# Weight sums of batch 1 on VectorE inside its own first layer, and the rest of a first layer begun one gap earlier

## The chip, the cores and the metric

One core of one Trainium2 chip. The metric is the device time of one execution in microseconds (us). The engines are TensorE (PE; PEld is its weight load), VectorE (DVE), ScalarE (ACT), GpSimd (POOL) and SyncE (SP), which issues most DMAs. Each engine works through its own instructions in the order of the program and waits on semaphores for the others.

## What is computed

```
mask   = q_assign[:, :, :, None] == k_assign[:, :, None, :]   # 16 clusters a head
scores = where(mask, q @ k.T / 8, -1e9);  attn = softmax(scores)
x = (attn @ v).transpose(0, 2, 1, 3).reshape(3072, 512)       # 4 batches of 768 rows
h = x @ w_in                                                  # 512 x 2048
g = h * (1.0 / (1.0 + exp(-1.702 * h)))
out = g @ w_out                                               # 2048 x 512
```

q, k and v are (4, 8, 768, 64). The first layer of the feed-forward part is `x @ w_in` with its gelu, the second is `g @ w_out`.

## The kernel before

The attention of all 16 pairs of heads comes first (to 339.85 us). Then the four batches follow one another, a first and a second layer each, and TensorE's order is this order. The kernel writes every engine's order by hand: instructions run on an engine in the order in which the Python code issues them, and small generators (`nxt`, `more`, `rest`, `pend`) are advanced at chosen places so that VectorE's work falls between TensorE's products.

Both layers use seven products of sums in place of eight blocks (Winograd's form of Strassen's method). A product needs sums of weight blocks and sums of the moving operand, made beforehand by VectorE or GpSimd, and its result is added to or copied from a PSUM bank by VectorE (`add`, L884) and ScalarE (copies, gelus).

- **First layer, batch 0** (`first7`, L893): seven products for each f of 8. `sums_w` makes the weight sums S1, S2, S4 of a later f on GpSimd.
- **First layer, batch 1** (`first7_psum`, L928): for each of 8 steps n, with f = `TURN[n]`, seven products accumulate in three banks x, z, v: A11 to x (copied to g1), A12 to z (added by VectorE to g1), S2 onto x (copied by ScalarE), S1 to v (copied by ScalarE), S3 onto x (added), S4 onto v (added), A22 onto x. ScalarE's order in a step is: copy x, copy x, gelu of the sum with z, copy v, two gelus, the last gelu. `sums_w1(n + 2)` (L977) issues the three sums S2, S1, S4 of step n + 2, all on GpSimd; for n = 0 and 1 they go to tiles W and are issued in batch 0's first layer, for n = 2 to 7 into parts of Z2, Z1 and Z2 again, tiles that hold weight sums of the second layer at other times. In steps n = 2, 4, 6 and after the last, `inner_w` (L994) makes sums of those sums on VectorE, eight instructions, and stores them and the sums of the two steps before to DRAM (`kept_i`, L1017, four DMAs issued by SP), where batches 2 and 3 get them.
- **First layer, batches 2 and 3** (`first49`, products L1083 and L1128): two levels, 49 products. It leaves a generator `rest`: the last additions (L884) and gelus (L1068), in two steps. The first is one addition of G, four of banks m to G, and two gelus.
- **Second layer, all batches** (`second49`, L1253): seven outer products k, in `ORDER`, each of seven inner ones: 1 to bank x, 2 to bank z, 6 onto x, 5 to v, 7 onto x, 3 onto v, 4 onto x. After the first, ScalarE copies x (L1263); after the second VectorE adds z, then `extra(0)` is called; after 6 ScalarE copies x again (L1269), so that 7 can be added; after 7 and 3 come `extra(1)` and `extra(2)`. `extra` advances `nxt` (the temporaries t2, t1, t4 of the next outer product, on VectorE), `more`, and in the first outer product `rest`, at 0 and at 1.

GpSimd's order behind batch 0's first layer is: four sums of Y (outputs, 128x768) in batch 0's second layer, then the 18 sums of `sums_w1` for n = 2 to 7, then batch 1's sums of Y. The sums for n = 6 write blocks of Z2 that `inner_w` of step 4 has just had stored to `kept_i`.

`sums` (L618) is the helper that records every such sum, so its line is that of many instructions; the tile names tell them apart.

Of the kernel before, what the change touches and what calls it, by code (L numbers as in the profile page):

```python
# [38 lines left out]
def fast(  # L39
# [26 lines left out]
    nc = tc.nc  # L66

    B, H, S, D = q.shape
# [547 lines left out]
    def sums(engine, todo):  # L616
        for o, a, op, b in todo:
            engine.tensor_tensor(out=o, in0=a, in1=b, op=(  # L618
                ALU.add if op == "+" else ALU.subtract))
# [3 lines left out]
    def A_in(row, col, f):  # L623

        at = (row * FB + f) * P
        return w_in[:, 2 * col:2 * col + 2, at:at + P]
# [182 lines left out]
    def turn_w(i):  # L809
        a = W_of(i)  # L810
        sums(nc.vector, ((a(0, 1), a(0, 0), "-", a(0, 1)),))
# [71 lines left out]
    def add(o, p, a):  # L883
        nc.vector.tensor_tensor(out=o, in0=p, in1=a, op=ALU.add)  # L884
# [92 lines left out]
    def sums_w1(n):  # L977

        if n >= FB:
            return  # L980
        f = TURN[n]
        if n < 2:
            S = wq.tile([P, 3, 2, P], FP32, name="W")
        else:
            S = Zb[1 + n // 2 % 2][:, n % 2 * 6:n % 2 * 6 + 6].rearrange(
                "p (i c) n -> p i c n", c=2)
        w_of[FB + f] = {1: S[:, 0], 2: S[:, 1], 3: A_in(1, 0, f), 4: S[:, 2],
                        0: S}
        S = w_of[FB + f]
        A11, A12, A22 = A_in(0, 0, f), A_in(0, 1, f), A_in(1, 1, f)  # L990
        sums(nc.gpsimd, ((S[2], A22, "-", S[3]), (S[1], S[2], "+", A11),
                         (S[4], A12, "-", S[2])))

    def inner_w(j, S):  # L994

# [243 lines left out]
    def second49(k, extra, last):  # L1239

        i = ORDER[k]
        a, g, t, w = W_of(i), G_of(i), temps(k), W.pop(k)
        A = {1: a(0, 0), 2: a(1, 0), 3: w[:, 2], 4: a(1, 1), 5: w[:, 1],
             6: w[:, 0], 7: a(0, 1)}
        M = {1: g(0, 0), 2: g(1, 0), 3: g(1, 1), 4: t[4], 5: t[1], 6: t[2],
             7: t[3]}

        def bank_b():
            return ps_b.tile([P, 512], FP32, name="b")[:, 0:QT]

        def product(ps, n, start):
            for f in range(FQ):
                nc.tensor.matmul(out=ps, lhsT=A[n][:, f], rhs=M[n][:, f],  # L1253
                                 start=start and f == 0,
                                 stop=(f == FQ - 1), skip_group_check=True)

        y = Y[22] if i == 1 else ep.tile([P, 2, HALF], FP32, name="y")
        y11, y12, y21, y22 = (y[:, m, q * QT:(q + 1) * QT]
                              for m in range(2) for q in range(2))
        p5 = ep.tile([P, QT], FP32, name="p5")  # L1260
        x = bank_b()
        product(x, 1, True)
        nc.scalar.copy(y11, x)  # L1263
        z = bank_b()
        product(z, 2, True)
        add(y11, z, y11)
        extra(0)
        product(x, 6, False)
        nc.scalar.copy(y12, x)  # L1269
        v = bank_b()  # L1270
        product(v, 5, True)
        nc.scalar.copy(p5, v)
        product(x, 7, False)
        nc.scalar.copy(y22, x)
        add(y22, y22, p5)
        extra(1)
        product(v, 3, False)
        add(y12, v, y12)
        if i == 4:
            c = Y[21]  # L1280
            add(c[:, 0], y[:, 0], c[:, 0])
            add(c[:, 1, QT:], y22, c[:, 1, QT:])
            extra(2)
        product(x, 4, False)
        if i == 4:
            add(c[:, 1, 0:QT], x, c[:, 1, 0:QT])
            return
        nc.scalar.copy(y21, x)
        extra(2)
        pool = nc.vector if last and i in (5, 7) else nc.gpsimd  # L1290
        sums(pool, {1: (),
                    2: ((Y[11], y, "+", Y[22]),),
                    3: ((Y[12], y, "+", Y[22]),),
                    6: ((Y[12], y, "+", Y[12]), (Y[21], y, "+", Y[22])),
                    5: ((Y[12], y, "+", Y[12]), (Y[22], y, "+", Y[21])),
                    7: ((Y[22], y, "+", Y[22]), (Y[21], y, "+", Y[21]))}[i])
# [74 lines left out]
    def do(steps, n):  # L1371
        for _ in range(n):
            next(steps, None)
# [3 lines left out]
    for b in range(B):  # L1377
        if b == 1:
            done = None
            for n, f in enumerate(TURN):  # L1380
                made_w = w_of[FB + f][0]
                first7_psum(b, f, *XT)
                if n % 2 == 0 and done:
                    inner_w(*done)
                sums_w1(n + 2)
                if n:
                    after7(TURN[n - 1])
                if n % 2 == 0:
                    one = made_w
                else:  # L1390
                    done = f - FQ, (one, made_w)
                do(pend, 2)
            after7(FB - 1)
            inner_w(*done)
        if b > 1:
            rest = first49(*XT)
        for f in range(FB if b == 0 else 0):
            first7(b, f, *XT)
            if f + 2 < FB:
                sums_w(f + 2)  # L1400
            else:
                sums_w1(f + 2 - FB)
            if f:
                after7(f - 1)
            if b == 0 and f < 3:
                for n in range(3 * f, min(3 * f + 3, FB)):
                    sums_z((nc.gpsimd, nc.vector, nc.vector)[n % 3], n)
            if b == 0 and f in (3, 4):
                for i in ORDER[0:4] if f == 3 else ORDER[4:]:
                    turn_w(i)  # L1410
            if b == 0 and f >= 3:
                for k in {3: (0,), 4: (1, 2), 5: (3,), 6: (4,), 7: ()}[f]:
                    keep_w(k, spare_y())
                if 5 <= f < 7:
                    load_sums(f - 5)
        if b == 0:
            after7(FB - 1)
        if b:
            move_z(b, 0)
        if b < B - 1:  # L1420
            for h in range(2):
                for hp in range(HP):
                    x = xT_of[b + 1, h, hp] = xp.tile([P, HALF], FP32,
                                                      name="x")
            made = sums_x(b + 1)
        else:
            made = iter(())

        def stores(b, *todo, **how):
            for n in todo:  # L1430
                store(b, n, **how)
                yield

        def tail():
            store(b, 22)
            yield

        def chain(*todo):
            for steps in todo:
                yield from steps  # L1440

        def sums_of_x():
            for XT[:] in made:
                yield

        x_steps = sums_of_x()
        final = b == B - 1
        if b < 2:
            rest = iter(())

        for k in range(7):
            nxt = sums_t(k + 1) if k < 6 else iter(())
            more = {1: sums_G(6), 2: sums_G(5), 3: sums_G(4),
                    4: stores(b, 11), 5: stores(b, 12) if final else x_steps,
                    6: tail() if final else x_steps}.get(k, iter(()))
            if b == B - 1 and k < 2:
                test(k)
            if (b, k) == (B - 1, 6):
                is_bad = nc.values_load(bad[0:1, 0:1], min_val=0, max_val=1)

            def extra(at):
                if k == 0 and at < 2:
                    do(rest, 1)
                do(nxt, (2, 1, 1)[at])
                do(more, ((1, 0, 1) if final else (0, 4, 4))[at] if k == 6
                   else (0, 0, 4)[at] if k == 2 else (0, 2, 2)[at])

            second49(k, extra, b in (0, B - 1))
            if k < 5:
                load_sums(k + 2, b == 0 and k > 2)  # L1470
            elif b < B - 1:
                load_sums(k - 5)
            if k < 3 and not (k == 2 and b):
                move_z(b, k + (b > 0))
            if k == 2 and b < B - 1:
                for h in range(2):
                    for hp in range(HP):
                        nc.sync.dma_start(out=xT_of[b + 1, h, hp],
                                          in_=kept[b, h, hp])
            if k in (4, 5) and 0 < b < B - 1:  # L1480
                load_inner(k - 4)
        pend = () if final else stores(b, 12, 22, 21)
        if final:
            store_last(b)
# [439 lines left out]
```

## Time and profile before

| | us |
|---|---|
| runs of the kernel | 894.80, 894.53, 893.81, 894.86; median 894.67 |
| the profiled execution, its own time | 893.86 |
| its span, first to last instruction | 892.1 |

Stages by TensorE's timeline, with the busy time of each engine in them:

| stage | from | to | length | PE | DVE | ACT | POOL |
|---|---|---|---|---|---|---|---|
| attention | 0 | 339.85 | 339.85 | 337.53 | 299.21 | 238.31 | 313.07 |
| batch 0, first layer | 339.85 | 412.13 | 72.28 | 72.28 | 65.45 | 21.16 | 58.23 |
| batch 0, second layer | 412.13 | 481.25 | 69.12 | 64.71 | 63.33 | 12.23 | 24.27 |
| batch 1, first layer | 481.25 | 553.50 | 72.25 | 72.25 | 35.29 | 26.67 | 4.55 |
| batch 1, second layer | 553.50 | 617.36 | 63.86 | 63.86 | 58.97 | 11.36 | 20.92 |
| batch 2, first layer | 617.36 | 684.82 | 67.46 | 67.46 | 41.82 | 28.87 | 0.00 |
| batch 2, second layer | 684.82 | 750.58 | 65.76 | 63.94 | 60.57 | 13.17 | 20.90 |
| batch 3, first layer | 750.58 | 818.21 | 67.63 | 67.63 | 41.99 | 28.86 | 0.00 |
| batch 3, second layer and end | 818.21 | 892.10 | 73.89 | 65.09 | 59.12 | 14.11 | 11.60 |

The granted clock of TensorE is 0.998 of full speed over the span. A line of a timeline reads: start and duration in us, engine, line of the program, operation, output<-inputs by the names of the program's tiles, shapes, number of instructions merged, and in brackets the idle time of the engine just before with what ended it. Durations overlap a little, since an instruction begins before its forerunner has left the engine; distances from start to start are the pace. An engine that is idle costs nothing unless TensorE comes to wait for it.

### The profile page before, as it was taken

The numbers are of one execution on the slowest core, as the hardware profiler recorded it, in microseconds if no ns is written. First come the engines' busy times: TensorE is split into PE (matmuls) and PEld (weight loads), VectorE is DVE, ScalarE is ACT, GpSimd is POOL, SyncE is SP. The second block draws the span as 40 slices with busy tenths as digits, with TensorE's granted clock in tenths as the row PEclk, the third lists the DMA queues.
The fourth block names the chain that finished last, engine by engine and source line by source line (L and its number), as shares of the span: only waits on it lengthen the run. The fifth ranks groups of instructions, "written<-read, shape, count | busy, mean of one in ns | idle before, by whom it ended". The sixth has DMA issues, their size and how long they took to land.

```text
span 892.1 us, 18225 instructions
## 1 busy us (share of the span) xinstructions
PE 874.7 (98%) x6910; PEld 605.1 (68%) x6910; DVE 725.8 (81%) x1223; ACT 394.7 (44%) x868; POOL 453.5 (51%) x411
## 2 busy tenths in 40 slices
PE   8999999999999999999989999999999999999996
PEld 3444444444444445557987556999887999887996
DVE  4899898999999996998898445799665899665895
ACT  3677777777677774322112333112434212444211
POOL 6899999999999997694270001144000143000140
PEclk9999999999999999999999999999999999999999
DMA  9655566656655320034633331747501547501424
GB/s 179 126 108 105 104 121 146 138 134 137 139 130 122 87 67 19 0 118 158 227 110 114 74 121 71 283 142 267 172 24 48 165 143 265 172 25 48 165 75 108
DMA packets 183186, 110.49 MB, mean 124 GB/s; under 512 B 153528, under 2 KB 161712, under 8 KB 180528
## 3 DMA queue, kind: packets, MB, share of 16 engines
q1 hardware_dynamic: 182832, 109.09, 45.0%
q8 instruction: 57, 0.93, 0.5%
q14 instruction: 41, 0.34, 0.1%
q10 hardware_dynamic: 256, 0.13, 0.1%
HBM read 83.05 MB, written 26.14 MB: 122 GB/s over the span
## 4 chain that ended last, share of the span: by engine, by line
PE 92%; DVE 6%; issue 1%; ACT 0%; POOL 0%; DVEq 0%; ACTq 0%; POOLq 0%
PE b L1253 23%; PE s L492 14%; PE o L557 14%; PE b L1128 8%; PE b L928 8%; PE b L893 8%; PE m L1083 7%; PE s L515 3%; PE m L574 3%; DVE G L618 2%; PE m L348 1%; DVE E L618 1%; DVE G L884 1%; PE o L296 1%; DVE Wz L618 0%
## 5 line engine op out<-in xcount | busy, mean ns | idle before, releaser
L541 POOL TENSOR_TENSOR sum<-sum,A 128x384 f32<-128x384 f32 x252 | 265.3, 1089 | 23.3 <-ACT A L523 21.7
L618 POOL TENSOR_TENSOR Y<-y,Y 128x768 f32<-128x768 f32 x24 | 63.3, 2651 | 307.5 <-DVE y L884 277.0
L523 ACT ACTIVATE A<-s 128x768 f32<-128x768 f32 x192 | 146.2, 807 | 85.8 <-PE s L515 66.4
L492 PE MATMUL s<-T,T 64*64 64x384 f32 x1536 | 143.1, 487 | 0.0
L557 PE MATMUL o<-A,inv 64*64 64x384 f32 x1536 | 141.2, 483 | 0.0
L884 DVE TENSOR_TENSOR G<-b,G 128x384 f32<-128x384 f32 x128 | 68.4, 554 | 57.9 <-PE b L928 36.2
L492 PEld LDWEIGHTS s<-T,T 64*64 64x64 f32 x1536 | 54.9, 132 | 69.1 <-ACT A L523 35.8
L618 DVE TENSOR_TENSOR G<-G 128x768 f32<-128x768 f32 (+1 forms) x84 | 96.3, 1173 | 0.2
L557 PEld LDWEIGHTS o<-A,inv 64*64 64x64 f32 x1536 | 58.3, 133 | 38.4 <-issue 33.3
L1253 PE MATMUL b<-G,w_out 128*128 128x192 f32 x320 | 55.9, 326 | 0.0
L1253 PEld LDWEIGHTS b<-G,w_out 128*128 128x128 f32 x320 | 52.7, 190 | 1.1
L1141 ACT COPY G<-b 128x384 f32<-128x384 f32 x64 | 30.4, 479 | 52.2 <-PE b L1128 52.2
L1253 PE MATMUL b<-E,Wz 128*128 128x192 f32 x288 | 50.5, 327 | 2.1 <-DVE E L618 2.1
L1253 PEld LDWEIGHTS b<-E,Wz 128*128 128x128 f32 x288 | 47.2, 190 | 3.0 <-issue 1.8
L515 PE MATMUL s<-rows,rows 64*64 64x384 bf16 x720 | 45.5, 322 | 0.0
L515 PEld LDWEIGHTS <-rows 64*64 64x64 bf16 x720 | 23.0, 107 | 32.7 <-issue 32.6
L1253 PE MATMUL b<-G,Wz 128*128 128x192 f32 x224 | 41.0, 326 | 0.0
L1253 PE MATMUL b<-G,Z 128*128 128x192 f32 x224 | 39.0, 326 | 0.0
L618 POOL TENSOR_TENSOR Z<-w_in 128x256 f32<-128x256 f32 x6 | 6.3, 1057 | 63.3 <-DVE G L884 63.3
L541 POOL TENSOR_TENSOR sum<-A 128x384 f32<-128x384 f32 x32 | 37.2, 1186 | 0.0
L1253 PEld LDWEIGHTS b<-G,Wz 128*128 128x128 f32 x224 | 37.2, 190 | 0.0
L1253 PEld LDWEIGHTS b<-G,Z 128*128 128x128 f32 x224 | 36.8, 190 | 0.0
(237 smaller groups left out, 1713.5 us busy)
## 6 DMA issues: line engine op xcount, KB each, us to landing
Wz<-kept_w SPq DMA_DIRECT2D x78, 256.0 KB
Z<-kept_z SPq DMA_DIRECT2D x9, 1024.0 KB
raw<-in_moe_w_in_dram SPq DMA_DIRECT2D x16, 512.0 KB
raw<-in_moe_w_out_dram SPq DMA_DIRECT2D x16, 512.0 KB
Z<-kept_i SPq DMA_DIRECT2D x8, 1024.0 KB
inv<-in_v_dram SPq DMA_DIRECT2D x16, 384.0 KB
in<-in_q_dram SPq DMA_DIRECT2D x60, 96.0 KB
in<-in_k_dram SPq DMA_DIRECT2D x60, 96.0 KB
```

The lines of the kernel that those rows point to most:

```text
L492: nc.tensor.matmul(out=ps[c:c + D, a, 0:HALF], lhsT=T[p, 1][rows, kt * P + c:kt * P + c + D], rhs=T[p, 0][rows, h * HALF:(h + 1) * HALF], ...
L515: nc.tensor.matmul(out=s_of[u][c:c + D, a, :], lhsT=rows_of[1, p % 2][rows, kt * P + c:kt * P + c + D], rhs=rows_of[0, p % 2][rows, h * HA ...
L523: nc.scalar.activation(out=A_of[u], in_=s_of.pop(u), func=AF.Exp, scale=SCALE)
L541: nc.gpsimd.tensor_tensor(out=sum_of[g][:, a], in0=(A_of[u - 1] if kt == 1 else sum_of[g])[:, a], in1=A_of[u][:, a], op=ALU.add)
L557: nc.tensor.matmul(out=o_of[g][a * D:(a + 1) * D, r, 0:HALF], lhsT=v_in[p][rows, a, kt, :], rhs=A[rows, a, :], start=(kt == 0), stop=(kt = ...
L618: engine.tensor_tensor(out=o, in0=a, in1=b, op=(ALU.add if op == "+" else ALU.subtract))
L884: nc.vector.tensor_tensor(out=o, in0=p, in1=a, op=ALU.add)
L893: nc.tensor.matmul(out=ps[:, 0:HALF], lhsT=a[:, c], rhs=x(c), start=(c == 0), stop=(c == 1))
L928: nc.tensor.matmul(out=ps, lhsT=a[:, c], rhs=x(c), start=start and c == 0, stop=(c == 1), skip_group_check=True)
L1083: nc.tensor.matmul(out=whole_of[j][m][:, 0:HALF], lhsT=a[:, c], rhs=x(c), start=n == 1 and c == 0, stop=c == 1, skip_group_check=True)
L1128: nc.tensor.matmul(out=ps[i][:, h * QT:(h + 1) * QT], lhsT=a(o), rhs=M[o][n], start=n in (1, 2, 5) and h == 0, stop=True, skip_group_check ...
L1253: nc.tensor.matmul(out=ps, lhsT=A[n][:, f], rhs=M[n][:, f], start=start and f == 0, stop=(f == FQ - 1), skip_group_check=True)
```

## The change

1. The 18 sums of `sums_w1` for n = 2 to 7 are made by VectorE. They are issued where they were issued before, after `inner_w` of the step if it has one, but in VectorE's order instead of GpSimd's. The six sums for n = 0 and 1 stay on GpSimd. No DMA is added or removed, and SP's order is the same.
2. In the first outer product of a second layer the first step of `rest` is taken at a new call, `extra(-1)`, between ScalarE's copy of x and the product to z, so that it stands ahead of VectorE's addition of z instead of behind it. The second step is taken at `extra(1)` as before. Only batches 2 and 3 have a `rest`. The orders of TensorE and ScalarE stay the same.

```diff
@@ sums_w1
         A11, A12, A22 = A_in(0, 0, f), A_in(0, 1, f), A_in(1, 1, f)
-        sums(nc.gpsimd, ((S[2], A22, "-", S[3]), (S[1], S[2], "+", A11),
-                         (S[4], A12, "-", S[2])))
+        sums(nc.gpsimd if n < 2 else nc.vector, (
+            (S[2], A22, "-", S[3]), (S[1], S[2], "+", A11),
+            (S[4], A12, "-", S[2])))
@@ second49
         x = bank_b()
         product(x, 1, True)
         nc.scalar.copy(y11, x)
+        extra(-1)
         z = bank_b()
         product(z, 2, True)
         add(y11, z, y11)
@@ extra
             def extra(at):
-                if k == 0 and at < 2:
+                if k == 0 and at % 2:
                     do(rest, 1)
+                if at < 0:
+                    return
                 do(nxt, (2, 1, 1)[at])
```

## The prediction

> **What bounds the kernel now.** I read the page first, then the chain of waits, then each engine's timeline where the edits land.
>
> ```profile
> PE 874.7 (98%) x6910; PEld 605.1 (68%) x6910; DVE 725.8 (81%) x1223; ACT 394.7 (44%) x868; POOL 453.5 (51%) x411
> ...
> PE 92%; DVE 6%; issue 1%; ACT 0%; POOL 0%; DVEq 0%; ACTq 0%; POOLq 0%
> ```
>
> TensorE sets the end; only where it stands idle can this change gain, and only a new idle time of TensorE can cost. In the timeline of TensorE the feed-forward part has five gaps that matter here. Three lie in batch 0's second layer:
>
> ```profile
> 463.00 1.54 PE L1253 MATMUL b<-Tx,Wz 128*128 128x192 f32 x8 [2.29 <-DVE Tx L618]
> 465.11 1.57 PE L1253 MATMUL b<-E,Wz 128*128 128x192 f32 x8 [0.57 <-DVE E L618]
> ...
> 474.68 2.84 PE L1253 MATMUL b<-E,Wz 128*128 128x192 f32 x16 [1.50 <-DVE E L618]
> ```
>
> The bracket is the idle time and who ended it: VectorE, late with the temporaries of an inner product. Two, of equal length, open the second layers of batches 2 and 3 (batch 2's is shown below). Batch 1's first layer (481.25 to 553.50) has no gap: TensorE 72.25 us of 72.25, VectorE 35.29.
>
> **Edit 1, what goes: twelve GpSimd sums in batch 0's second layer.** GpSimd runs them without pause from 455.80 to 470.54. VectorE's instructions are longer in just that time. Its timeline, three sums of one form in a row, the first begun while GpSimd still worked:
>
> ```profile
> 469.87 1.21 DVE L618 TENSOR_TENSOR Wz<-w_out 128x512 f32<-128x512 f32 x1
> 471.12 0.69 DVE L618 TENSOR_TENSOR Wz<-Wz,w_out 128x512 f32<-128x512 f32 x1
> 471.73 0.68 DVE L618 TENSOR_TENSOR Wz<-w_out,Wz 128x512 f32<-128x512 f32 x1
> ```
>
> From 456.57 to 471.12 VectorE is never idle and takes 14.55 us. At the pace of its own rows without GpSimd the same instructions take: three Wz sums 1.94 (0.73 + 0.61 + 0.60, start to start), G and Tx 0.98 + 0.87 (as at 445.74), two E 0.87 + 0.89, two Y 1.74 (as the G pair at 448.73), two transposes 0.95, three short y sums 0.27 + 0.27 + 0.25, the next Wz 0.73: 9.76 us. VectorE gains 4.79 us.
>
> What is late next? Up to the end of Tx it gains 2.15 (Wz 1.47, G 0.27, Tx 0.41), so Tx ends at 460.71 and TensorE goes on 0.14 later, as now, at 460.85. Without a stall it would get there at 457.95 + 2 x 1.30 = 460.55: 0.30 stays, and 0.08 for starting again (1.54 instead of 1.46 in the row). The E of the third gap ends at 474.55 - 4.79 = 469.76; TensorE wants it at 470.03. So the next layer begins at 457.95 + 14 x 1.30 (two outer products of seven) + 0.38 = 476.53 instead of 481.25: **-4.72 us** (at most 5.10 with no stall at all, at least some 4.4 if VectorE's pace stays a little worse). GpSimd's own sums of Y up to 455.84 stay, so the slow VectorE rows before that stay.
>
> [...] VectorE and GpSimd instructions overlap here and VectorE's take 1.2 to 1.8 times as long. [...]
>
> **Edit 1, what comes: 18 sums on VectorE in batch 1's first layer.** The form is there already in `inner_w` (Z<-w_in, 0.42 us; starts 0.46, 0.34, 0.33 apart), so one step's three sums cost 1.13. For the steps n = 0, 1, 3 and 5 they fall into idle time of VectorE: it ends at 492.7 before the addition at 493.14, at 501.3 before 502.17, at 518.4 before 520.23, and likewise at n = 5. Nothing.
>
> At n = 2 and n = 4 they stand behind the eight sums of `inner_w`, where VectorE is already late. This is what queues there, at n = 4, on VectorE, ScalarE and TensorE:
>
> ```profile
> 528.63 0.42 DVE L618 TENSOR_TENSOR Z<-w_in,Z 128x256 f32<-128x256 f32 x1
> 528.97 0.55 DVE L618 TENSOR_TENSOR G<-G 128x384 f32<-128x384 f32 x1
> ...
> 530.76 0.55 DVE L884 TENSOR_TENSOR G<-b,G 128x384 f32<-128x384 f32 x1
> ```
> ```profile
> 531.34 0.52 ACT L936 ACTIVATE G<-G 128x384 f32<-128x384 f32 x1 [0.39 <-DVE G L884]
> 531.77 0.47 ACT L949 COPY G<-b 128x384 f32<-128x384 f32 x1
> ```
> ```profile
> 532.86 1.45 PE L928 MATMUL b<-x,Z 128*128 128x384 f32 x4
> ```
>
> The addition at 530.76 feeds a gelu, behind it in ScalarE's order stands the copy of the bank v, and TensorE's product with S4 (532.86) may not write v before. The copy ends at 532.24, plus 0.15 to TensorE (copy to matmul at 691.86 and 692.01): slack 0.47. At n = 2 the times are 18.07 earlier and the same. There 1.13 more makes the addition end at 514.38, the copy at 515.31, the product start at 515.46 instead of 514.79: 0.67, plus 0.08: **+0.75 us**.
>
> At n = 4 the sums go into the first six blocks of Z2, which a DMA to `kept_i`, issued just before, is still reading. In the changed program's instruction list the first of them waits on that DMA. GpSimd waited for the same now, at no cost:
>
> ```profile
> 529.08 3.04 SPq L1017 DMA_DIRECT2D kept_i<-Z  x4
> ```
> ```profile
> 533.79 0.73 POOL L618 TENSOR_TENSOR Z<-w_in 128x256 f32<-128x256 f32 x1 [63.26 <-DVE G L884]
> ```
>
> The profile names VectorE, long done; the queues moved 256 GB/s until 534.0 and 25 after, so the release is the landing. On VectorE this wait blocks the whole order behind it: released at 533.8 instead of going on at 528.97, then the three sums (1.13), then G, Y and E as now (1.79), so the addition starts at 536.7 and ends 537.25. Gelu, copy (ends 538.18), product with S4 at 538.33 instead of 532.86: 5.47, plus 0.08: **+5.55 us**. Bounds: nothing if the wait is over by then (below nothing is excluded, since nothing is taken from this stage's path); 0.7 more if the release comes only with the last of the four pieces (the queues are quiet by 534.5). I take the GpSimd row, since it is the same wait. No other queue gets longer: SP's order is the same, and GpSimd loses 18 instructions.
>
> **Edit 2: the rest of a first layer, batches 2 and 3.** Its five additions now stand behind a sum that waits for TensorE's second product:
>
> ```profile
> 687.70 0.36 DVE L884 TENSOR_TENSOR Y<-b,Y 128x192 f32<-128x192 f32 x1 [1.79 <-PE b L1253]
> 687.97 0.95 DVE L884 TENSOR_TENSOR G<-G 128x768 f32<-128x768 f32 x1
> 688.84 1.95 DVE L884 TENSOR_TENSOR G<-m,G 128x384 f32<-128x384 f32 x4
> ```
> ```profile
> 689.95 1.71 ACT L1068 ACTIVATE G<-G 128x768 f32<-128x768 f32 x2 [3.30 <-DVE G L884]
> 691.56 0.30 ACT L1269 COPY Y<-b 128x192 f32<-128x192 f32 x1
> ```
> ```profile
> 692.01 1.54 PE L1253 MATMUL b<-Y,w_out 128*128 128x192 f32 x8 [1.82 <-ACT Y L1269]
> ```
>
> Additions, two gelus, the copy of x, and TensorE, which adds to x again, hang in one chain. Put ahead of the waiting sum, the additions start when VectorE is free, at 685.82 (their inputs are there: TensorE's last first-layer product ends at 684.98): 2.15 earlier. The second gelu ends at 689.5, the copy at 689.75, TensorE may go on at 689.9 and wants to at 687.42 + 2.60 = 690.02. The gap closes: 1.99 + 0.08 = **-2.07 us**. The sum moved back ends at 688.9; nobody waits for its bank soon. In batch 3 two instructions of the check stand ahead (VectorE free at 819.70, not 821.36): 1.66 earlier, TensorE at 823.75 instead of 825.40: **-1.65 us**, with 0.34 left. VectorE runs close behind TensorE later in these layers, but from a wait for ScalarE at 703.04, so it moves along.
>
> **Sum.** -4.72 + 0.75 + 5.55 - 2.07 - 1.65 = **-2.14 us** against the profiled execution's 893.86 (span 892.1, 1.8 around it): 891.7. That execution lies 0.81 under the median of the runs, 894.67; against the median it is **892.5**, which I give. Own range 891.0 (no stall left at 460, no gap in batch 3) to 893.9 (slower release, smaller first gain).
>
> **Rivals.**
> 1. *No wait at n = 4* (the DMA has read its piece when VectorE gets there). The step then costs 0.75 like n = 2: 892.5 - 4.8 = 887.7. Against it: VectorE is there 0.1 us after the issue, and the piece is 384 KB behind one of 896.
> 2. *Edit 2 does not do what it says*: the copy or the gelus wait for something else. Then 3.72 is missing: 896.2. Against it: no other wait stands in the rows.
> 3. *Slower:* VectorE is not slowed by GpSimd at 456 to 471 but by something that stays, such as DMA traffic. The 4.72 is missing: 897.2. It decides as soon as under 2.6 of the 4.72 comes. Against it: the pace changes at 470.54, with GpSimd's last instruction, while the DMA share rises (0.28 before 471.2, 0.79 after).
>
> **Chances.** My forecast 0.74 (0.49 of it faster by over 0.2%, 0.25 within), rival 1 0.08, rival 2 0.06 (half within, half slower), rival 3 0.06, unforeseen 0.06 (0.01 faster, 0.01 within, 0.04 slower). About 0.2%, 1.8 us, is what a measurement of this kernel can tell from no change. Faster 0.58, within 0.29, slower 0.13. The range 890.0 to 896.3 leaves out rivals 1 and 3 and part of the unforeseen.
>
> **What would show it.** After: no GpSimd row between 456 and the next batch's Y sums; Wz rows of 0.69; a gap of TensorE before 462 of about 0.3 and none in the product after; batch 1's first layer 78.5 us long instead of 72.25, with one gap near 5.5 (at the product with S4 of the sixth step) and one near 0.7; the gap that opens batch 2's second layer gone and batch 3's at 0.3. A first layer of under 75 us, or Wz rows still at 1.2, makes the forecast wrong.

## The result, and the profile after

The changed kernel takes 895.53 us (median of 38 runs, 894.33 to 897.27), the kernel before 893.54 (58 runs in all, 892.17 to 896.2). The ratio, from runs side by side, is 1.0018 [1.0014, 1.0023]: slower by about 1.6 us. The forecast was 892.5, a gain. The profiled execution of the changed kernel took 895.01 with a span of 892.8; before, 893.86 and 892.1. All differences below between two profiles are between such executions.

**TensorE gets faster, the program does not.** The page's busy times and the chain that ended last:

```profile
PE 875.1 (98%) x6910; PEld 605.2 (68%) x6910; DVE 727.7 (82%) x1241; ACT 394.6 (44%) x868; POOL 434.7 (49%) x393
...
PE 94%; DVE 2%; DMA 1%; ACT 1%; issue 0%; SPq 0%; DVEq 0%; ACTq 0%
```

The 18 sums have gone from POOL (411 to 393) to DVE. In the chain TensorE has 94% instead of 92, VectorE 2 instead of 6, so waits for VectorE did vanish. DMA stands in it anew: 4.21 us of it are the store to `kept_i` (525.22 to 529.43), as much again the loading of k at the program's start. TensorE's last matmul ends at 884.23, 0.89 *earlier* than before (885.12). The span ends 0.77 *later*. Both halves need an explanation.

**What came as forecast.** VectorE's timeline in batch 0's second layer, the three Wz sums that had taken 1.21, 0.69 and 0.68, and TensorE's where its gap of 2.29 was and at the end of the layer:

```profile
465.38 0.69 DVE L618 TENSOR_TENSOR Wz<-w_out 128x512 f32<-128x512 f32 x1
466.10 0.69 DVE L618 TENSOR_TENSOR Wz<-Wz,w_out 128x512 f32<-128x512 f32 x1
466.71 0.69 DVE L618 TENSOR_TENSOR Wz<-w_out,Wz 128x512 f32<-128x512 f32 x1
```
```profile
457.90 2.76 PE L1254 MATMUL b<-G,w_out 128*128 128x192 f32 x16
460.68 1.54 PE L1254 MATMUL b<-Tx,Wz 128*128 128x192 f32 x8
...
476.36 2.74 PE L928 MATMUL b<-x,w_in 128*128 128x384 f32 x8
```

Two products take 2.60, so 460.68 is 0.18 late: a rest of a gap, as forecast (0.30). The other two gaps are gone, and the next layer begins at 476.36 instead of 481.25. In the layers of edit 2, TensorE's third product no longer waits in batch 2 (692.87 is 2.60 after 690.27), and keeps 0.30 in batch 3 (824.50 is 2.90 after 821.60):

```profile
690.27 2.76 PE L1254 MATMUL b<-E,Wz 128*128 128x192 f32 x16
692.87 1.46 PE L1254 MATMUL b<-Y,w_out 128*128 128x192 f32 x8
...
821.60 2.76 PE L1254 MATMUL b<-E,Wz 128*128 128x192 f32 x16
824.50 1.54 PE L1254 MATMUL b<-Y,w_out 128*128 128x192 f32 x8
```

**What did not.** Batch 1's first layer is 79.99 us long, not 78.5. VectorE's, then TensorE's timeline at the sums of n = 6 (issued in step n = 4):

```profile
529.46 0.42 DVE L618 TENSOR_TENSOR Z<-w_in 128x256 f32<-128x256 f32 x1 [4.63 <-DMA kept_i<-Z]
529.91 0.42 DVE L618 TENSOR_TENSOR Z<-Z,w_in 128x256 f32<-128x256 f32 x1
```
```profile
527.33 1.45 PE L928 MATMUL b<-Tx,w_in 128*128 128x384 f32 x4
533.91 2.69 PE L928 MATMUL b<-x,Z 128*128 128x384 f32 x4 [5.12 <-ACT G L949]
536.39 2.06 PE L928 MATMUL b<-Tx,w_in 128*128 128x384 f32 x4
538.28 2.74 PE L928 MATMUL b<-x,w_in 128*128 128x384 f32 x8
```

The wait is there, behind the named DMA, and the gap is the forecast one: without it the product with S4 would start 1.29 after 527.33, so 5.29 are lost (forecast 5.47 + 0.08). But the next two products, of four matmuls each, start 2.48 and 1.89 apart instead of 1.29. Windows over this stretch (each engine's busy time, then the granted clock, the DMA share, GB/s) tell why:

```profile
526.00:528.62 2.62, 2.62 (x9) 1.33 (x7) 0.00 (x0) 0.48 (x1) 0.00 (x0) 1.00 0.99 395
...
533.91:536.40 2.49, 2.49 (x5) 1.30 (x6) 0.54 (x1) 0.52 (x1) 0.00 (x0) 0.56 0.00 0
536.40:537.30 0.90, 0.90 (x3) 0.59 (x2) 0.67 (x2) 0.08 (x1) 0.00 (x0) 0.50 0.00 0
537.30:538.30 1.00, 1.00 (x4) 0.46 (x4) 0.97 (x4) 0.45 (x1) 0.00 (x0) 0.85 0.02 8
```

TensorE is busy all the time but at half clock. The trace's record of the clock, of which the views print only means, has half speed from 534.19 for 3.41 us; before, it has none inside the work. The two products lose 1.79.

**TensorE's account** adds up: -4.89 (first gain) + 0.67 (n = 2) + 5.29 (gap at n = 4) + 1.79 (clock) - 2.06 and - 1.68 (second layers of batches 2 and 3, 65.76 to 63.70 and, up to the matmuls that transpose the last output, 65.87 to 64.19) = -0.88, against -0.89 measured.

**The rest lies behind TensorE.** From its last matmul to the end of the span it is 6.94 us before and 8.60 after; from the span to the execution's own time 1.80 and 2.18. The last packet of output lands at 888.48 before and at 887.73 after, so it is not the output. SyncE closes the program: after a branch it goes through a row of semaphore instructions 0.06 to 0.10 apart. In the changed kernel it stands still after the sixth, from 889.69 to 891.34. Before, it nowhere pauses in that row. (These rows are in the packed trace's list of instructions; the views leave semaphore instructions out.)

### The profile page after: what moved, and what is told of

Read it like the earlier page. It is cut to its first block, busy times and chain, and to the rows that moved or that the text cites. A ratio compares the mean times of both kernels' runs of the same rounds, so it can differ in the third digit from the quotient of the medians.

```text
span 892.8 us, 18197 instructions
## 1 busy us (share of the span) xinstructions
PE 875.1 (98%) x6910; PEld 605.2 (68%) x6910; DVE 727.7 (82%) x1241; ACT 394.6 (44%) x868; POOL 434.7 (49%) x393
## 4 chain that ended last, share of the span: by engine, by line
PE 94%; DVE 2%; DMA 1%; ACT 1%; issue 0%; SPq 0%; DVEq 0%; ACTq 0%
PE b L1254 28%; PE s L492 14%; PE o L557 14%; PE b L1129 8%; PE b L893 8%; PE m L1084 7%; PE b L928 7%; PE s L515 3%; PE m L574 3%; PE m L348 1%; DVE Z L618 1%; DVE G L884 1%; DMA in<-in_k_dram 1%; DMA in<-in_q_dram 0%; DMA kept_i<-Z 0%; DVE E L618 0%
## 5 line engine op out<-in xcount | busy, mean ns | idle before, releaser
L618 DVE TENSOR_TENSOR G<-G 128x768 f32<-128x768 f32 (+1 forms) x84 | 94.3, 1150 | 0.2
L898 ACT ACTIVATE G<-G 128x384 f32<-128x384 f32 x32 | 16.1, 523 | 46.5 <-DVE G L884 45.2
```

Of the source, the lines that this page charges most:

```text
L618: engine.tensor_tensor(out=o, in0=a, in1=b, op=(ALU.add if op == "+" else ALU.subtract))
```

## The experiments

Theory 1: the lost time in batch 1 is VectorE's wait behind the DMA to `kept_i` *and* the half clock that TensorE's idle time brings. Its rival: matmuls after the gap are slow because VectorE and ScalarE catch up beside them on the same memory. Theory 2, formed from the first four runs: SyncE's pause comes from the length of its own program (872 recorded instructions before, 863 after; nine fewer waits, the same 605 transfers), which moves the place of the pause; that SyncE waits there for a piece of its code is the author's guess. Its rival: the end is longer because of what the change does to transfers or to the clock. In the expectations theory 1 is called A and theory 2 D; B says that 18 more sums are too much work for VectorE wherever they stand, and C that edit 2 costs, outside TensorE's path.

Each kernel was timed beside the kernel before: 893.32 for the first four, 893.71 for the others.

### Edit 1 alone

The kernel before, with the first part of the diff only.

> Edit 1 alone; the rest of a first layer stays where it was. Theory A (VectorE's wait for the DMA at n = 4 idles TensorE 5.3 us, and after that idle time TensorE runs some microseconds at half clock): 1.6 + 3.7 = 5.3 us slower than before (ratio 1.006), the slow matmuls behind the gap of 5.1 us are there again, and the gaps that open the second layers of batches 2 and 3 are 1.8 us as before. Theory B (the 18 sums are too much work for VectorE wherever they stand): the same total, but with further gaps in other steps. Theory C (edit 2 is what costs, outside TensorE's path): equal to or faster than before.

Measured: 899.42, ratio 1.0065 [1.0051, 1.0078], 6.1 slower (5.3 was expected). TensorE ends at 888.57, 3.45 later than before in the profiles; the rest lies behind it. The same gap, and a longer half clock: 531.84 for 6.83 us.

```profile
533.82 2.92 PE L928 MATMUL b<-x,Z 128*128 128x384 f32 x4 [5.13 <-ACT G L949]
536.54 2.51 PE L928 MATMUL b<-Tx,w_in 128*128 128x384 f32 x4
```

The half clock began in the gap and ran to 538.67, 4.85 us behind the gap's end; half of that is 2.43. The layer is 80.69 long, 0.70 more than in the changed kernel, which had 3.41 us, half of it 1.71. So in these two profiles the clock's price is half of what is left of the slow time when TensorE starts again.

### Edit 2 alone

The changed kernel with the sums back on GpSimd:

```diff
-        sums(nc.gpsimd if n < 2 else nc.vector, (
-            (S[2], A22, "-", S[3]), (S[1], S[2], "+", A11),
-            (S[4], A12, "-", S[2])))
+        sums(nc.gpsimd, ((S[2], A22, "-", S[3]), (S[1], S[2], "+", A11),
+                         (S[4], A12, "-", S[2])))
```

> Edit 2 alone; the 18 sums stay on GpSimd. Theories A and B: 3.7 us faster than before (2.05 + 1.69, the two gaps of the profile after), ratio 0.996, granted clock as before. Theory C: slower than before.

Measured: 889.66, ratio 0.9958 [0.9945, 0.9972], 3.66 faster. Both terms of edit 2 were right (the two second layers are 63.70 and 64.18 long), and theory C falls. SyncE has 872 instructions here, and the closing row has no pause. The clock was not as before: there is one stretch of half clock, from 462.24 for 3.41 us, at the old gap in batch 0's second layer.

```profile
462.45 2.90 PE L1253 MATMUL b<-Tx,Wz 128*128 128x192 f32 x8 [2.28 <-DVE Tx L618]
465.15 1.72 PE L1253 MATMUL b<-E,Wz 128*128 128x192 f32 x8
...
474.13 2.84 PE L1253 MATMUL b<-E,Wz 128*128 128x192 f32 x16 [0.76 <-DVE E L618]
```

It cost nothing, since TensorE then waits less for VectorE (0 and 0.76 instead of 0.57 and 1.50): the layer is 69.11 long, and 69.13 before.

### A tile of its own for the sums of n = 6

Both edits; the sums that waited go to a tile W that no DMA reads.

```diff
-        if n < 2:
+        if n < 2 or n == 6:
             S = wq.tile([P, 3, 2, P], FP32, name="W")
```

> Both edits, but the sums of step n = 6 go to a W tile in place of the blocks of Z2 that a DMA is still reading; their place in VectorE's order and their number are unchanged. Theory A: no wait, no idle time of 5 us, no half clock; n = 4 then costs 0.67 as n = 2 does, and the time is 4.9 + 3.7 - 2 x 0.67 = 7.3 us less than before (ratio 0.992). Theory B: the sums are all still there, so about the time of the changed kernel, 1.6 us over before, or at most 2 us less than that.

Measured: 888.63, ratio 0.9946 [0.9932, 0.9959], 4.7 faster. In TensorE's timeline only the two small gaps are left, and no half clock lies inside the work:

```profile
510.88 1.56 PE L928 MATMUL b<-x,Z 128*128 128x384 f32 x4 [0.40 <-ACT G L949]
...
529.60 1.56 PE L928 MATMUL b<-x,Z 128*128 128x384 f32 x4 [0.39 <-ACT G L949]
```

Theory B falls: the same sums stand in the same places. TensorE ends at 878.23, 6.89 earlier than before, near the 7.3 expected of the whole, but the total gained 2.6 less than expected. Most of that difference is the end of the program again: 8.72 instead of 6.94, and 2.2 instead of 1.8 outside the span. SyncE has 864 instructions, one more than the changed kernel, and pauses one closing instruction earlier, after the fifth (883.27 to 885.38). This made theory 2.

### TensorE kept busy in the gap

Both edits, and in the sixth step 22 extra matmuls into a bank that nothing reads, ahead of the product with S4.

```diff
         product(x, S[3], lambda c: T[3, c], False)
+        if f == TURN[5]:
+            spare = bank()
+            for _ in range(22):
+                nc.tensor.matmul(
+                    out=spare, lhsT=ident_h,
+                    rhs=ident_h[:, None, :].broadcast_to((P, 4, P)),
+                    start=True, stop=True)
         add(g2[:, 1], x, g2[:, 1])
```

> Both edits, and 22 matmuls 128x512 bf16 of the identity into a spare bank between the products with S3 and S4 of the sixth step, so that TensorE has work while it would wait (about 4.8 us at full clock); work is only added. Theory A: the wait stays 5.3 us long, but the product behind it runs at full pace (1.29 per step and not 2.48 and 1.89), the mean granted clock is that of before, and the time is 0.9 + 1.8 = 2.7 us less than before (ratio 0.997); more than the 1.8 us of the profile against the changed kernel if ordinary runs lose more by the clock than the profiled one. If the clock plays no part: equal to the changed kernel or slower, 1.6 us over before.

Measured: 893.20, ratio 0.9997 [0.9988, 1.0006]; 2.3 under the changed kernel's median (1.9 by the two ratios), though work was only added. The gain of 2.7 over the kernel before did not come. TensorE's timeline and a window behind the gap:

```profile
528.59 4.91 PE L954 MATMUL m<-ident_h 128*128 128x512 bf16 x22
533.87 1.56 PE L928 MATMUL b<-x,Z 128*128 128x384 f32 x4 [0.37 <-ACT G L949]
535.27 1.45 PE L928 MATMUL b<-Tx,w_in 128*128 128x384 f32 x4
```
```profile
534.00:537.00 3.00, 3.00 (x10) 1.81 (x11) 1.91 (x5) 1.29 (x3) 0.00 (x0) 1.00 0.01 3
```

The product with S4 starts as late as in the changed kernel (533.87 against 533.91), VectorE and ScalarE catch up beside it here too, and the matmuls run at full pace (the next product starts 1.40 later, not 2.48, at a granted clock of 1.00). So it is the clock, and not the neighbours; the rival of theory 1 falls. TensorE ends at 882.50, 2.62 earlier than before; against the kernel before nearly the whole of it is lost at the program's end, which theory 1 left out.

Half clock lasted 3.41 us in the changed kernel's profile, 6.83, twice that, in that of edit 1 alone. In all ten profiles every change of the clock lies a whole number of stretches of 3.413 us, called windows here, behind the first one (155 and 156 in the changed kernel, 154 and 156 with edit 1 alone, 134 and 135 with edit 2 alone), wherever the gap is. A gap need not fill a window: if the span is divided by this grid, each window at full clock of which TensorE's matmuls, by their recorded times, left 60% or more idle was followed by half clock (92% in the changed kernel, 60% at the gap of 2.28 with edit 2 alone), and none with 58% or less was (58% at the start of the changed kernel's gap, 55% at the gap of 2.29 in the kernel before). With edit 1 alone, the first slow window was itself 58% idle, and a second slow one followed. So for 2.3 us of idleness it was a matter of its place on the grid, while 5.12 us leave at least one window 75% idle wherever they fall (half of 5.12, over 3.413): by these figures, an estimate from the ten profiles, half clock was to be expected behind it; one window of it came in the changed kernel's profile, two in that of edit 1 alone.

### All sums on VectorE, issued where it has time

Both edits, with the sums moved to steps that have no `inner_w`. The sums of n = 6 then come long after the store.

```diff
-                sums_w1(n + 2)
+                for m in {0: (2,), 1: (3, 4), 3: (5,), 5: (6, 7)}.get(n, ()):
+                    sums_w1(m)
```

> Both edits, all 18 sums on VectorE, but issued where VectorE has idle time and no DMA is in the way: step 0 issues the sums for n = 2, step 1 those for 3 and 4, step 3 those for 5, step 5 those for 6 and 7; none stand behind the sums of sums. Theory A (the place behind the DMA costs, not the work): no gap of TensorE in batch 1's first layer (length 72.25 us), its gains stay at 4.9 + 3.7 = 8.6 us, less about 2.3 us that a pause in SyncE's closing instructions takes as in the runs before: 6.3 us faster than before, ratio 0.993. Theory B (the work costs): not faster than the own buffer, 4.7 us.

Measured: 886.92, ratio 0.9924 [0.991, 0.9937], 6.8 faster. VectorE does six sums in a row, none of them behind a DMA, and waits for TensorE again soon after (0.65), not TensorE for it; batch 1's first layer is 72.24 long:

```profile
529.59 0.41 DVE L618 TENSOR_TENSOR Z<-w_in 128x256 f32<-128x256 f32 x1
...
531.51 0.42 DVE L618 TENSOR_TENSOR Z<-w_in,Z 128x256 f32<-128x256 f32 x1
531.85 0.55 DVE L618 TENSOR_TENSOR G<-G 128x384 f32<-128x384 f32 x1
533.05 0.56 DVE L884 TENSOR_TENSOR G<-b,G 128x384 f32<-128x384 f32 x1 [0.65 <-PE b L928]
```

### Only the last six sums left on GpSimd

```diff
-        sums(nc.gpsimd if n < 2 else nc.vector, (
+        sums(nc.gpsimd if n < 2 or n > 5 else nc.vector, (
```

> Both edits, but the sums for n = 6 and 7 stay on GpSimd, which may wait for the DMA at no cost. Theory A: one gap of 0.6 in batch 1's first layer (n = 2), none of 5, and 4.9 + 3.7 - 0.7 - 2.3 = 5.6 us faster than before, ratio 0.9937. SyncE's program is three instructions longer than in the changed kernel, so its closing pause should come after the third closing instruction and not after the sixth.

Measured: 887.69, ratio 0.9928 [0.9914, 0.9941], 6.0 faster. The gap of n = 2 stays (511.67, 0.40 idle); the one of n = 4 is away, with the same sums in the same tile behind the same DMA, only on an engine for which nobody waits. SyncE has 866 instructions, three more than the changed kernel, and pauses after the third closing instruction (883.22 to 885.25).

### Eight more instructions on SyncE

The changed kernel with the three stores of batch 0's sums to `kept_z` cut into four pieces each: nine more transfers of the same bytes, and one wait fewer.

```diff
-        nc.sync.dma_start(out=o, in_=i)
+        parts = 1 if b else 4
+        for at in range(0, FB, FB // parts):
+            nc.sync.dma_start(out=o[:, at:at + FB // parts],
+                              in_=i[:, at:at + FB // parts])
```

> The changed kernel with the three stores to kept_z cut into four pieces each, which makes SyncE's program 8 instructions longer and moves the same bytes. Theory D (the 2 us between TensorE's end and the program's end are a load of SyncE's code at a fixed place of its program): the pause among the closing instructions is gone, the end comes about 6.5 to 7 us after TensorE's last product and not 8.6, and the time is about 2.3 us under the changed kernel, 0.4 under before (ratio 0.9996). Rival (the end waits for the last stores, or for other engines): the same time as the changed kernel.

Measured: 893.23, ratio 0.999 [0.9981, 1.0]; 2.3 under the changed kernel. TensorE ends where it did (884.03 against 884.23), with the same gap and half clock for 3.41 us:

```profile
533.71 2.84 PE L928 MATMUL b<-x,Z 128*128 128x384 f32 x4 [5.15 <-ACT G L949]
536.34 1.91 PE L928 MATMUL b<-Tx,w_in 128*128 128x384 f32 x4
```

The end is 7.41 instead of 8.60 long, 1.8 instead of 2.2 lie outside the span, and there is no pause in the closing row. Besides the number of SyncE's instructions only the pieces of three stores in batch 0 are different, so theory 2 stands and its rival falls: clock and transfers near the end are as they were.

### Sums moved, and the eight instructions

The last two diffs together.

> The moved sums of e5 with the longer program of SyncE of e7. Theories A and D together: 8.6 us faster than before, ratio 0.9904, the full sum of TensorE's gaps. If D is wrong: as e5.

Measured: 885.23, ratio 0.9902 [0.9887, 0.9917], 8.5 faster: the fastest of all versions. Its chain of waits, and a window over batch 1's first layer:

```profile
PE 97%; DVE 1%; DMA 0%; SPq 0%; issue 0%; ACT 0%; ACTq 0%; DVEq 0%
```
```profile
476.08:548.32 72.24, 72.24 (x226) 42.56 (x226) 41.35 (x99) 26.72 (x55) 0.00 (x0) 1.00 0.28 93
```

### The end of the program, all kernels side by side

| kernel | SyncE's instructions | pause after closing instruction | its length | last matmul to end of span | outside the span |
|---|---|---|---|---|---|
| before | 872 | none | | 6.94 | 1.80 |
| edit 2 alone | 872 | none | | 6.21 | 1.80 |
| changed, + 8 | 871 | none | | 7.41 | 1.79 |
| moved, + 8 | 871 | none | | 7.31 | 1.80 |
| last six on GpSimd | 866 | 3rd | 2.03 | 8.63 | 1.80 |
| own tile | 864 | 5th | 2.11 | 8.72 | 2.18 |
| changed | 863 | 6th | 1.65 | 8.60 | 2.18 |
| edit 1 alone | 863 | 6th | 2.01 | 8.73 | 2.18 |
| kept busy | 863 | 6th | 2.03 | 8.96 | 2.17 |
| sums moved | 863 | 6th | 1.77 | 8.61 | 2.18 |

The pause moves by one place for each instruction: the two numbers add to 869 wherever it shows. With 871 or 872 it would fall ahead of the first closing instruction, where SyncE spends 2.6 to 3.1 us behind its branch in those kernels and 2.5 to 2.6 in those with the pause, so that it would be hidden nearly whole there. The queue table of each of these profiles has two queues of kind "instruction": one with 57 packets of 16384 bytes, one with 40 or 41, mostly of 8192. SyncE has 863 of the 18,197 recorded instructions of the changed kernel, 5%, so by that share, an estimate, most of the 57 can hardly be its own. In each of the six pauses a packet of the second queue starts, 0.15 to 0.42 us after the last instruction ahead of the pause, and has ended 1.1 to 1.5 us before SyncE goes on; but such packets come about every microsecond there, in the kernels without a pause too. That the pause is a wait for a piece of code is the author's guess from this, not shown: the trace doesn't say what SyncE waits for, nor which queue brings its code. What is shown is its place and its length, 1.65 to 2.11 us.

## Why the prediction was wrong

| step | forecast | measured |
|---|---|---|
| edit 1, first gain | -4.72 | -4.89 |
| the sums at n = 2 | +0.75 | +0.67 |
| the wait at n = 4, gap | +5.55 | +5.29 |
| ... and what follows it | 0 | +1.79 (clock) |
| edit 2, batch 2 | -2.07 | -2.06 |
| edit 2, batch 3 | -1.65 | -1.68 |
| end of the program | 0 | +1.66 in the span, +0.38 outside |
| sum | -2.14 | +1.16 (own times: 1.15) |

- **Right:** every gap, its cause and, within 0.3 us, its size: GpSimd's sums slowed VectorE (in the seven other profiles with edit 1 batch 0's second layer is 64.37 to 64.39 long, 4.74 to 4.76 less than before), the DMA's landing releases VectorE at n = 4, the copy at L949 passes the wait on to TensorE, and the additions of `rest` alone opened the two second layers. None of the three rivals came: the wait at n = 4 exists, edit 2 does what it says (-3.66 by itself), and VectorE speeds up.
- **Failed, first:** the term "Gelu, copy (ends 538.18), product with S4 at 538.33 instead of 532.86: 5.47, plus 0.08". It took TensorE to go on after 5 us of idleness at its old pace but for 0.08. That is true of the gaps of 0.4 and, in the profile of before, 2.29; after 5.12 it was 1.79, shown by the run in which busy matmuls filled the same gap and took the loss away. The bounds given for the step (nothing to 0.7 more) dealt only with the release. In the changed kernel's runs the price varies: those with a mean clock of 0.996, that of the profiled execution with its one slow window, have a median of 894.66, those at 0.994 of 895.19 and those at 0.993 of 895.89. That these had two windows is inferred from the profile of edit 1 alone (6.83 us, mean clock 0.994).
- **Failed, second:** "against the profiled execution's 893.86 (span 892.1, 1.8 around it)" carried everything after the last matmul over unchanged. "SP's order is the same" was true, and its length was not: nine waits fell away, and with 863 instructions a pause falls into SyncE's closing row. That this belongs to SyncE's instructions is shown by the run with eight more of them (2.3 less, TensorE as before).
- Either failure alone would have left about no change: by the account -0.88 with the clock and -0.63 with the end; the two kernels that take one of them away stand at 0.9997 and 0.999. Both together gave the loss. The range (890.0 to 896.3) held the time by luck: none of the cases behind it named either mechanism. And the 892.5 stood on four runs of the kernel before, whose median of 894.67 lies 1.1 above that of all 58.
- **Open:** the 0.38 outside the span. It goes with 863 and 864 instructions and not with 866, though that kernel has the pause as well; what lies there the profile doesn't record.

## What to carry to other kernels

An engine that others wait for should not be given an instruction that waits for a DMA: that wait cost TensorE 5.29 here, without the clock; the same sums cost 0.66 when they went to another tile, and nothing on GpSimd or one step later. Price a new gap of TensorE with what follows it: behind 5 us of idleness came one or two slow windows of 3.41 us here, 1.8 to 2.5 us more in the profiles. And when a sum of gaps explains TensorE's end but not the time, look at what is behind its last matmul: removing nine waits on SyncE made this program end 2 us later.

## What the runs showed of the hardware that was not expected

- TensorE at half clock in whole windows of 3.41 us, whose place against the gap is not the same in two profiles (from 534.19 behind a gap that ends at 533.91, from 531.84 in one that ends at 533.82); even 2.28 us of idleness, which left 60% of one window idle, was followed by one in one execution. Extra matmuls in the gap kept the clock at 1.00 and were worth about 2 us (1.9 to 2.3).
- A pause of 1.65 to 2.11 us in SyncE's closing instructions whose place moves one for one with the number of its instructions.
- Wz sums of VectorE that take 0.69 alone took 2.19 and 2.30 in the changed kernel's profile (454.00 to 458.42) beside GpSimd's two sums of Y, and these took 6.93 instead of 4.85: both engines' instructions got longer. In the kernel before and in all eight other kernels it was the two sums of G ahead of them that were longer (5.05 instead of 1.82) beside the same sums of Y, and these took 4.85: which instructions got longer was not the same in all executions.
